# First two quads of an attention and projection kernel on two hardware queues, with a searched schedule

## The chip, the cores and the metric

One core of a Trainium2 chip. The time is the device time of one execution in microseconds (us), measured over whole launches; the profiled span is a little shorter than it. The kernel before takes 432.91 us (median of 3 runs, 432.63 to 433.24) and its profiled span is 431.5 us.

Engines in the text: PE is TensorE's matmul (PEld its weight load), ACT is ScalarE, DVE is VectorE, POOL is GpSimd, SP is SyncE, which only issues transfers here.

## The reference

```python
# q, k, v: (8 batches, 12 heads, 448 positions, 64), float32
def _attn_ref(q, k, v):
    scores = np.matmul(q, k.transpose(0, 1, 3, 2)) / np.sqrt(64)
    m = np.max(scores, axis=-1, keepdims=True)
    e = np.exp(scores - m)
    attn = e / (np.sum(e, axis=-1, keepdims=True) + np.exp(-m) + 1e-09)
    return np.matmul(attn, v)

# x: (3584 tokens, 768), w_in: (768, 2048), w_out: (2048, 768)
def _moe_ref(x, w_in, w_out, a, b):
    h = x @ w_in
    P = a[0] + a[1] * h + a[2] * h**2 + a[3] * h**3
    Q = 1.0 + abs(b[0]) * abs(h) + abs(b[1]) * h**2
    return (P / (Q + 1e-06)) @ w_out
# x is the attention's output, heads side by side; the result is (3584, 768) float32
```

## The kernel before

Each batch is worked as three "quads" of four heads. A quad's Q and K are loaded, transposed (by PE for the first six quads, later by DMA), multiplied into scores, put through Exp on ACT, and multiplied with ones (the sums) and with V (the values). A group of scores, its Exp and so on is an entry in a queue of its engine; `Plan` simulates the engines with fixed durations and writes the instructions in the order that this simulation gives. So the constants below are not measured at run time: they decide, when the kernel is built, in which order each engine works. PE has attention, first projection ("gemm1", `x @ w_in`) and second product ("gemm2", by `w_out`) to interleave; until the first sums of batch 0 are multiplied in, it has only attention.

```python
DUES = (0, 0, 4, 6); T0 = 18.0; T1 = 22.0; P1 = 1.3; LEAD = 45.0   # due times of a quad's scores
def quad_due(n):
    if n < 2 * NQ:
        return T1 + 8 * P1 * (n - NQ)
    return T0 + 8 * PER * (n - NQ)

def first_loads():                    # quad 0, in eight pieces of 112 KB, float32
    # ... piece(ti, pr, jh, nj, dma, lat, cast): ti 0 = K, 1 = Q; a load on queue `dma`
    #     into a stage, and a cast to float16 by the engine `cast`
    piece(0, 0, 0, 2, "ACT", 2.8, "ACT")
    piece(1, 0, 0, 2, "SP", 2.65, "DVE")
    piece(0, 0, 2, 2, "ACT", 3.4, "ACT")
    piece(1, 1, 0, 2, "SP", 3.9, "DVE")
    piece(0, 1, 0, 2, "ACT", 3.6, "ACT")
    piece(0, 1, 2, 2, "SP", 3.7, "ACT")
    for pr in range(2):
        piece(1, pr, 2, 2, "SP", 6.8, "DVE", True)     # second rows of Q, needed later

# ... transposes by PE: eight nc.tensor.transpose of 112 x 64 into one bank, one DVE copy out
# ... scores: tensor.matmul pairs on 64 rows each, Exp on ACT for 112 x 896 at a time
# ... attend: 16 sums, 2 x 16 values, Ln and Exp of the sums on ACT, two multiplies on DVE

# GpSimd's queue: quad 1 first (cast while loading), then the rest
kload.append(load_op(1, k, kn, "k", kfree, NN))
qload.append(load_op(1, q, qn, "q", qfree, NN))
loads(0, "v"); loads(2, "kq"); loads(1, "v"); loads(2, "v")
ORDER = "kq3 i kq4 i kq5 v3 i v4 i v5 o kq6 o o o"     # i, o: a group of weights
# ...
LAG = {0: (0, 2.67), 1: (5, 2), B - 2: (9, 2.67), B - 1: (8, 2)}   # places of second products
plan.run()
for op in plan.order:
    op.emit()
```

The softmax here doesn't subtract the row's maximum and nothing guards it: scores larger than these inputs give would overflow.

## Time and profile before

| | before |
|---|---|
| time, median of 3 | 432.91 us |
| profiled span | 431.5 us |
| PE busy | 419.2 us, 97% |
| ACT busy | 327.8 us, 76% |
| first Exp starts | 8.19 us |
| first sums start on PE | 13.93 us |
| first projection matmul starts | 27.30 us |
| from there to the end of the last second product | 400.9 us |

The page, the stretches of 5 us and the heads of the two timelines are shown in the prediction. Here is one more view, ACT's timeline between the first Exp and the first projection. The columns are start, busy time, engine, line, operation, out and in, shapes, number of instructions, and in brackets the idle time before the first of them and what ended it.

```profile
10.22 1.92 ACT L480 ACTIVATE e<-sps 112x896 f16<-112x896 f32 x2 [0.32 <-PE sps L472]
...
16.89 1.72 ACT L480 ACTIVATE e<-sps 112x896 f16<-112x896 f32 x2 [1.10 <-PE sps L472]
19.65 0.92 ACT L480 ACTIVATE e<-sps 112x896 f16<-112x896 f32 x1 [1.04 <-PE sps L472]
```

ACT waits for scores four times and for sums once, 3.5 us in all, before its chain runs dense from 19.65 us on.

### The profile page before, as it was taken

How to read it: one execution, taken by the hardware profiler on the slowest of the kernel's cores; microseconds unless marked ns; L12 is line 12 of the kernel's file. 1: busy time of each engine (PE TensorE's matmuls, PEld its weight loads, DVE VectorE, ACT ScalarE, POOL GpSimd, SP SyncE). 2: the span in 40 equal slices, each digit the busy share in tenths (PEclk: the TensorE clock that was granted, in tenths of full speed). 3: DMA queues.
4: the chain of work that ended last, by engine and by line, in shares of the span. 5: the costliest groups of instructions: out<-in, count | busy, mean ns of one | idle time of the engine just before them, and what ended most of it. 6: DMA issues, size and time to landing. Idle time of an engine off the chain costs nothing.

```text
span 431.5 us, 8834 instructions
## 1 busy us (share of the span) xinstructions
PE 419.2 (97%) x3680; PEld 218.7 (51%) x3680; DVE 339.9 (79%) x505; ACT 327.8 (76%) x386; POOL 120.7 (28%) x172
## 2 busy tenths in 40 slices
PE   3999999999999999999999999999999999999996
PEld 2667665544444444444454444444444455555563
DVE  2445999998999887698998668979698788999800
ACT  4699999798888777888886897877798854578521
POOL 5655516566005340423703333052000000000000
PEclk9999999999999999999999999999999999999999
DMA  9999999899606947299399886373211011111132
GB/s 148 202 200 205 207 180 150 152 154 162 123 2 69 160 85 118 28 141 115 58 117 107 119 123 85 81 108 73 45 36 38 2 36 38 36 38 36 39 103 81
DMA packets 78153, 43.12 MB, mean 100 GB/s; under 512 B 36128, under 2 KB 74528, under 8 KB 78112
## 3 DMA queue, kind: packets, MB, share of 16 engines
q0 software_dynamic: 37856, 22.35, 39.7%
q1 hardware_dynamic: 39472, 19.80, 25.5%
q8 instruction: 29, 0.48, 0.5%
q10 hardware_dynamic: 784, 0.39, 0.4%
q14 instruction: 12, 0.10, 0.1%
HBM read 45.62 MB, written 11.01 MB: 131 GB/s over the span
## 4 chain that ended last, share of the span: by engine, by line
PE 89%; ACT 4%; DMA 3%; DVE 1%; issue 1%; ACTq 0%; POOLq 0%
PE gen L671 34%; PE gen L573 33%; PE gen L507 12%; PE sps L472 10%; DMA kn<-in_k_dram 2%; ACT e L480 2%; DMA h<-in_k_dram 1%; ACT c L625 1%; ACT c L628 1%; PE gen L389 1%; DVE h L590 0%; ACT lden L521 0%; DVE x L535 0%; ACT lden L523 0%; DVE c L614 0%
## 5 line engine op out<-in xcount | busy, mean ns | idle before, releaser
L480 ACT ACTIVATE e<-sps 112x896 f16<-112x896 f32 x192 | 167.1, 917 | 41.5 <-PE sps L472 41.1
L573 PE MATMUL gen<-x,w_in 128*128 128x448 f16 (+1 forms) x864 | 161.8, 332 | 0.0
L671 PE MATMUL gen<-w_out,g 128*128 128x384 f16 (+2 forms) x768 | 135.9, 326 | 0.0
L573 PEld LDWEIGHTS <-w_in 128*128 128x128 f16 x864 | 79.9, 98 | 68.3 <-issue 14.4
L671 PEld LDWEIGHTS <-g 128*128 128x128 f16 x768 | 72.7, 98 | 58.4 <-issue 10.4
L590 DVE CAST h<-gen 128x448 f16<-128x448 f32 x113 | 69.4, 618 | 24.4 <-PE gen L573 24.3
L614 DVE TENSOR_TENSOR n<-n,h 128x1792 f16<-128x1792 f16 x64 | 70.1, 1095 | 0.7
L625 ACT ACTIVATE c<-c,oneeps_c 128x1792 f16<-128x1792 f16 x32 | 57.3, 1791 | 11.4 <-DVE c L614 11.1
L472 PE MATMUL sps<-qt,kt 64*128 64x448 f16 (+1 forms) x432 | 58.4, 343 | 2.3 <-ACT e L480 1.1
L648 POOL COPY gx<-g 128x1024 f16<-128x1024 f16 x8 | 8.3, 1040 | 183.1 <-DVE g L614 183.1
L693 ACT ACTIVATE o<-gen 128x384 f32<-128x384 f32 (+2 forms) x56 | 27.4, 490 | 36.2 <-PE gen L671 36.0
L628 ACT ACTIVATE c<-c 128x1792 f16<-128x1792 f16 x32 | 54.6, 1705 | 0.3
L610 DVE TENSOR_SCALAR n<-n,abc 128x1792 f16<-128x1792 f16 x64 | 44.3, 693 | 1.1
L614 DVE TENSOR_TENSOR g<-n,c 128x1792 f16<-128x1792 f16 x32 | 35.1, 1098 | 12.8 <-ACT c L628 11.5
L433 POOL COPY kp<-kn 112x256 uint32<-112x256 uint32 x36 | 26.1, 755 | 57.2 <-DMA kt<-kp 50.3
L507 PE MATMUL gen<-e,vn 112*32 112x448 f16 (+1 forms) x864 | 41.8, 337 | 0.0
L535 DVE TENSOR_TENSOR x<-gen,lden 128x448 f16<-128x448 f32 (+1 forms) x54 | 28.3, 563 | 13.9 <-ACT lden L523 12.7
L614 DVE TENSOR_TENSOR c<-c,w 128x1792 f16<-128x1792 f16 x32 | 35.2, 1100 | 0.0
L472 PEld LDWEIGHTS <-kt 64*128 64x128 f16 x432 | 15.0, 96 | 36.5 <-issue 32.9
L507 PEld LDWEIGHTS <-vn 112*32 112x32 f16 x864 | 23.1, 99 | 14.0
L433 POOL COPY qp<-qn 112x256 uint32<-112x256 uint32 x36 | 25.2, 726 | 18.1 <-DMA qt<-qp 18.0
L610 DVE TENSOR_SCALAR n<-h,abc 128x1792 f16<-128x1792 f16 x32 | 24.7, 772 | 0.1
(42 smaller groups left out, 248.1 us busy)
## 6 DMA issues: line engine op xcount, KB each, us to landing
vn<-in_v_dram POOLq DMA_DIRECT2D x24, 224.0 KB, 8.5
kn<-in_k_dram POOLq DMA_DIRECT2D x23, 224.0 KB, 5.7
qn<-in_q_dram POOLq DMA_DIRECT2D x23, 224.0 KB, 7.4
w_in<-in_moe_w_in_dram POOLq DMA_DIRECT2D x12, 256.0 KB, 9.7
w_out<-in_moe_w_out_dram POOLq DMA_DIRECT2D x4, 768.0 KB, 16.2
out_dram<-o SPq DMA_DIRECT2D x8, 336.0 KB, 3.2
out_dram<-o SPq DMA_DIRECT2D x8, 288.0 KB, 2.8
out_dram<-o SPq DMA_DIRECT2D x7, 240.0 KB, 2.5
```

The source lines that it names most:

```text
L433: nc.gpsimd.tensor_copy(out=mid[0].bitcast(U32)[:, pr], in_=src[n % NN].bitcast(U32)[:, 2 * pr:2 * pr + 2] .rearrange("p e j d -> p j e d"))
L472: nc.tensor.matmul(out=sps[m % NS][0:(P if i == 0 and j == 1 else 128), hh, ci * qw:(ci + 1) * qw], lhsT=kt[n % NK][r, c0:c0 + (P if i == ...
L480: nc.scalar.activation(out=e_sb[m % NE], in_=sps[m % NS][0:P, :, 0:S], func=AF.Exp, scale=scale)
L507: nc.tensor.matmul(out=gen[unit["bank"]][32 * h:32 * h + 32, 0:qw], lhsT=lhs(h, j), rhs=e_sb[m % NE][:, h % 2, c0:c0 + qw], start=(j == 0) ...
L535: mult.emit = lambda s=s, uu=uu: nc.vector.tensor_tensor(out=x_sb[b % NX][:, 2 * qd + s, q0:q0 + qw], in0=gen[uu["bank"]][:, 0:qw], in1=ld ...
L573: nc.tensor.matmul(out=gen[unit["bank"]][:, fi * qw:(fi + 1) * qw], lhsT=w_in_sb[wg][:, c // 2, c % 2, (fc % FG) * 128:(fc % FG + 1) * 128 ...
L590: nc.vector.tensor_copy(out=dst, in_=src)
L610: return lambda: nc.vector.tensor_scalar(out=out, in0=in0, scalar1=s1, scalar2=s2, op0=op0, **kw)
L614: return lambda: nc.vector.tensor_tensor(out=out, in0=in0, in1=in1, op=ALU.mult)
L625: lambda: nc.scalar.activation(out=c, in_=c, func=AF.Ln, bias=oneeps_c)))
L628: lambda: nc.scalar.activation(out=c, in_=c, func=AF.Exp, scale=-1.0)))
L671: nc.tensor.matmul(out=gen[unit["bank"]][:, 0:wd], lhsT=lhs, rhs=w_out_sb[f][:, fc % FG, cols], start=(fc == 0), stop=(fc == NFC - 1))
```

## The change

The intent: the first Exp comes earlier, since the first six pieces of Q and K meet no large load; quad 1 comes over the two hardware queues as float32 and is cast by DVE, while GpSimd's first load waits for a memset behind the first casts (`vz`); and from there on due times, the places of second products and the order of loads are found by search, against the plan's own model of the transfers (its constants are assumptions of the code).

```diff
-KB_US = 0.00252
+KB_US = 0.0027
+X_US = 1.3
+X_SHARE = 6.3
...
+    def transfer(self, op):
+        if op.kb < 0:
+            first = max(op.end + 0.3, self.ring)
+            behind = max(self.hbm - first, 0.0)
+            self.ring = first + X_US + min(behind, X_SHARE)
...
-    DUES = (0, 0, 4, 6)
-    T0 = 18.0
...
+    DUES = (0, 0, 4.2, 3.0)
+    LEAD = 50.9
+    DUE = (
+        28.1, 39.7, 51.4, 58.5, 76.4, 91.4, 103.2, 87.5, 118.5,
+        129.9, 148.0, 129.5, 202.0, 155.9, 169.8, 134.0, 237.8, 280.8,
+        283.4, 262.8, 327.3,
+    )
...
-        piece(0, 0, 0, 2, "ACT", 2.8, "ACT")
-        piece(1, 0, 0, 2, "SP", 2.65, "DVE")
-        piece(0, 0, 2, 2, "ACT", 3.4, "ACT")
...
+        plan.add("c0", piece(0, 0, 0, 2, "ACT", 2.8))
+        plan.add("c0", piece(1, 0, 0, 2, "SP", 2.65))
+        plan.add("c0", piece(0, 0, 2, 2, "ACT", 3.0, "ACT"))
+        piece(1, 1, 0, 2, "SP", 3.0)
+        piece(0, 1, 0, 2, "ACT", 3.4)
+        piece(0, 1, 2, 2, "SP", 3.4)
         for pr in range(2):
-            piece(1, pr, 2, 2, "SP", 6.8, "DVE", True)
+            for ti, (src, dst, dma) in enumerate(((k, kn, "ACT"), (q, qn, "SP"))):
+                stage = quad1_stage(ti, pr)
+                d = load(dma, src, 4 + 2 * pr, 2, stage, 0, J, 4.3 + 1.1 * pr)
+                cast(1, ti, pr, 0, J, dst[1][:, 2 * pr:2 * pr + 2], stage, d)
...
-    kload.append(load_op(1, k, kn, "k", kfree, NN))
-    qload.append(load_op(1, q, qn, "q", qfree, NN))
+    vz = plan.add("cpt", Op("vz", "DVE", 0.06, [first_casts[0, 1, 0, 0]],
+                            lambda: nc.vector.memset(vn[0][:, 0, 0, 0:2], 0.0)))
     loads(0, "v")
+    vload[0].deps.append(vz)
...
-    ORDER = "kq3 i kq4 i kq5 v3 i v4 i v5 o kq6 o o o"
+    ORDER = "kikiikivkkvoovoovkvv"
...
-            more = {-1: first[:2], 0: first[2:4], 1: first[4:], 2: nxt[:1], 3: nxt[1:2]}
+            more = {-1: first[:2], 0: first[2:3], 1: first[3:], 2: nxt[:2]}
...
-    LAG = {0: L0, 1: L1, B - 2: L6, B - 1: (8, 2)}
+    LAG = (
+        (0, 3.5), (12.0, 1.8), (6.5, 2.4), (5.0, 1.9),
+        (4.0, 3.4), (12.0, 1.8), (11.5, 2.8), (12.0, 1.3),
+    )
```

The rest of the diff is bookkeeping (lists turned into dictionaries, one load fewer in flight in the model).

## The prediction

> **What bounds the kernel now.** I read the page first, for which engine is full and where it is not:
>
> ```profile
> span 431.5 us, 8834 instructions
> PE 419.2 (97%) x3680; PEld 218.7 (51%) x3680; DVE 339.9 (79%) x505; ACT 327.8 (76%) x386; POOL 120.7 (28%) x172
> ...
> PE   3999999999999999999999999999999999999996
> ...
> PE 89%; ACT 4%; DMA 3%; DVE 1%; issue 1%; ACTq 0%; POOLq 0%
> ```
>
> PE is busy in 39 of 40 slices and holds 89% of the chain that ended last; DVE and ACT have a fifth to a quarter spare. Idle time lies in the first slice. Then busy time by stretches of 5 us (PE, PEld, DVE, ACT, POOL, clock, DMA share, GB/s):
>
> ```profile
> 0.00:5.00 5.00, 0.64 (x10) 0.52 (x12) 1.47 (x18) 2.12 (x3) 4.21 (x11) 1.00 0.50 123
> 5.00:10.00 5.00, 2.61 (x28) 1.21 (x27) 1.46 (x5) 2.33 (x4) 1.48 (x3) 1.00 1.27 167
> 10.00:15.00 5.00, 4.51 (x70) 2.99 (x72) 1.55 (x4) 3.63 (x5) 3.49 (x5) 1.00 1.38 200
> ```
>
> Half of the first 10 us is lost on PE, and by 15 us ACT has worked 8.1 us. The PE timeline shows what a busy PE does there:
>
> ```profile
> 8.03 0.40 PE L389 MATMUL gen<-ident,kn 112*64 112x112 f16 x4 [2.20 <-ACT kn L351]
> ...
> 12.18 0.93 PE L472 MATMUL sps<-qt,kt 64*128 64x224 f16 x8 [0.49 <-ACT e L480]
> ...
> 19.25 0.56 PE L472 MATMUL sps<-qt,kt 64*128 64x224 f16 x8
> ...
> 27.30 0.75 PE L573 MATMUL gen<-x,w_in 128*128 128x224 f16 x6
> ```
>
> The same eight score matmuls took 0.93 us at 12 us and 0.56 at 19 us: until about 18 us PE runs at half rate, though the page grants it the whole clock. The first projection matmul (L573) starts at 27.30; until then PE has only attention of batch 0 to do, and cannot be filled. What held ACT is in its own timeline, and the cause in the chain of the first 30 us:
>
> ```profile
> 4.41 0.42 ACT L351 ACTIVATE kn<-h 112x256 f16<-112x256 f32 x1 [0.47 <-DMA h<-in_k_dram]
> 7.56 0.72 ACT L351 ACTIVATE kn<-h 112x256 f16<-112x256 f32 x2 [2.74 <-DMA h<-in_k_dram]
> 8.19 1.70 ACT L480 ACTIVATE e<-sps 112x896 f16<-112x896 f32 x2
> ```
> ```profile
> 1.72 5.82 DMA h<-in_k_dram
> ...
> 10.01 8.87 DMA kn<-in_k_dram
> ```
>
> The first scores were written by 5.51 (PE starts them at 4.95), but ACT, in order, stood 2.74 us at a cast whose data landed only at 7.54. So the first exp began at 8.19.
>
> [...]
>
> **The change, part by part.** No matmul is added or removed. Array time is the same in both. At 2.4 GHz the first product is 8 x 16 x 6 x 448 columns = 143.36 us, the second the same, scores 35.84 (two row halves at once), sums and values 53.76 (four column groups), transposes 4.48: 380.8 us. Besides it PE pays for changes of kind: 9 projection matmuls from 203.97 to 205.68 pass into other projection matmuls almost without loss, but each step into or out of scores or values costs about 0.105 us (4 scores, 0.373 us of columns, take 0.48 to the next start). Counting steps in the built instruction order: 241 before, 234 after. That is 7 x 0.105 = 0.7 us gained, the whole of what the new places of second products can give by themselves.
>
> (a) Quad 1 goes from GpSimd's queue to the ACT and SP queues as f32, cast by DVE, and GpSimd's first load now waits for a DVE memset behind the first casts. So the six first pieces (0.69 MB) meet no large load. Pieces one to four landed by 4.4 in the trace; the other two should follow at about 5 instead of 7.2 to 7.5. Most casts go to DVE, which had worked 1.5 of 5 us; ACT keeps one cast, so nothing on it waits for a late piece. Against that, ACT issues two more DMAs (about 0.45 us each, from 0.74 to 2.2 now), so its table load of 1.28 us ends at 4.4 instead of 3.5: still before the first scores. First exp: about 5.7 instead of 8.19, a gain of 2.5 us.
>
> (b) From there ACT sets the pace until the first projection. In the built order that needs 14 exps and three pairs of ln and exp: 14 x 0.815 + 3 x (0.40 + 0.28) = 13.4 us, plus about 0.9 for PE and the last two multiplies. Before, 8.19 + 14.3 = 22.5 was possible and 27.30 came out: 4.8 us of slip, in ACT's gaps (1.10 and 1.04 us for scores) behind late loads and a PE at half rate. After, 5.7 + 14.3 = 20.0 is possible. Quad 2's Q and K are the second and third load of GpSimd instead of fourth and fifth. By the end of Q: 1.84 MB on the hardware queues and 3 x 0.459 MB; at the 0.39 MB/us that loads reach in the trace (one of 0.459 MB every 1.17 us) from 2.5 us on, 10.7 us against 14.54 now. The first weights: the same 6.6 MB in front of their last byte in both; 19.5 us by that rate against 23.45 measured. I leave a slip of 2.6 us for the half-rate PE and what isn't foreseen: first projection at **22.6**, a gain of 4.7.
>
> (c) From the first projection on PE has filling work. Before: 27.30 to 428.18 is 400.9 us, of which 370.9 are columns, 215 steps x 0.105 = 22.6, 1,760 projection matmuls x 2.5 ns = 4.4: 397.9. The rest, 3.0, is small losses and one hole of 1.1 us near 127 where ACT's exps were behind. After: 371.3 + 209 x 0.105 + 4.4 = 397.6. I put 2.4 for losses.
>
> Sum: 22.6 + 397.6 + 2.4 = 422.6; the last outputs as before, 431.5 - 428.2 = 3.3: span 425.9. Timed runs are 1.4 us over the profiled span (432.91 against 431.5): **427.3 us**, 1.3% faster.
>
> **Rivals.** First, the gain at the start is eaten by another wait. The weights may come late: between the first and the second weight group there are still Q and K of quad 4, and the sharing of quad 1's loads could slow everything else. For it: before 8.87 us only 1.15 MB had landed, well below the later rate, so the start isn't ruled by bytes alone. Against it: less is in flight in front of the bytes needed first. If the first projection stays at 25 or 26, the time is 430 to 431.
>
> Second, ACT becomes the bound later. The new due times pull attention forward. Weighing the instructions in program order with the durations of the trace, ACT has to do about 154 us by the time PE's own work reaches 160, against 144 before; in single 10 us stretches it is over 10. A hole like the one at 127 could come several times, 1 us each: 429 to 430. It speaks against this that in 40 to 60 us ACT was busy 9.3 and 9.9 of 10 us while PE had no gap.
>
> Third, it goes better: slip of only 1 us and losses down to 1 us. That gives 21.0 + 398.6 + 4.7 = 424.3, just at the line of 2%. Nothing else is there to take: without any loss after the start, and with PE full from 20 us, it is 422.
>
> **Range and chances.** The terms are independent: first projection 22.6 within about 1.5, losses 2.4 within about 1.5, and half a microsecond of run differences. That makes about 2.2 for one sigma-like error either way, and I widen it for the unforeseen: 424.2 to 430.6. Faster by over 2% (below 424.25) needs the third rival whole: 0.1. Slower by over 2% would need 9 us of new waits on a PE that has the same work: 0.01. Within 2%: 0.89.
>
> **What would show it.** First exp on ACT at 5.5 to 6.2; first projection on PE at 21 to 24; score groups of eight at 0.56 us from about 14 us instead of 19; PE's busy time in 5 to 10 us up from 2.61 to over 3.5. From the first projection to the last second product 399 to 401 us. If the first exp is near 8, step (a) is wrong; if it is early and the projection late, step (b); if the second length is over 402, ACT's holes are (c)'s fault and the waits of PE on scores will name them.

A paragraph is cut from the prediction where marked, since it restated rules that no run of this case had shown. 22.6 + 397.6 + 2.4 + 3.3 = 425.9, and 1.4 more is the 427.3. The trace of the kernel before shows this: K's first piece landed 2.7 us after its issue, and the third, issued at 1.72 us just behind GpSimd's first large load (1.49), took 5.8 us; that the large load held it up was the estimate. The column times of the sum can be read from the same trace: projection matmuls and second products of 224, 256, 384, 448 and 512 columns followed one another after 96, 109, 163, 189 and 216 ns (medians, at full rate). That is 0.417 ns for each column, the 2.4 GHz of the text, and 2.3 to 3.0 ns more for each matmul, the text's 2.5. The two matmuls of a pair of row halves (scores), and the four of a set of column groups (sums and values), started 3 ns apart (median).

## The result, and the profile after

The changed kernel takes 430.78 us (median of 4 runs, 430.65 to 431.20) against 432.77 for the kernel before in the same rounds (432.04 to 433.24, 4 runs). The ratio is 0.9957, 95% interval 0.9940 to 0.9974: 0.4% faster, where 1.3% was predicted. A ratio is here the mean time of one kernel's fast runs over the mean of the other's of the same rounds, so it is not quite the ratio of the two medians. The predicted class (within 2%) holds; the predicted time of 427.3 us and its range of 424.2 to 430.6 do not.

From the page of the kernel after: span and instructions, busy times, PE in 40 slices, and the chain by engine.

```profile
span 429.0 us, 8850 instructions
...
PE 418.3 (98%) x3680; PEld 218.5 (51%) x3680; DVE 339.7 (79%) x513; ACT 327.9 (76%) x383; POOL 109.3 (25%) x170
...
PE   5899999999999999999999999999999999999996
...
PE 81%; DVE 14%; ACT 2%; DMA 1%; issue 1%; ACTq 0%; DVEq 0%
```

Only the first two slices differ (5 and 8 in place of 3 and 9). The chain now passes through DVE for 14%, but no hole of PE belongs to that: PE is busy in all other slices as before. The busy times in stretches of 5 us (PE, PEld, DVE, ACT, POOL, clock, DMA share, GB/s) say where the early gain lies:

```profile
0.00:5.00 5.00, 0.60 (x8) 0.47 (x9) 1.48 (x21) 0.96 (x1) 1.17 (x7) 1.00 0.61 159
5.00:10.00 5.00, 4.08 (x48) 2.14 (x47) 3.11 (x12) 3.38 (x5) 4.80 (x8) 1.00 1.22 238
10.00:15.00 5.00, 4.55 (x76) 3.01 (x76) 2.01 (x6) 3.37 (x5) 3.06 (x5) 1.00 1.42 199
```

PE's busy time from 5 to 10 us rose from 2.61 to 4.08 us, with 48 matmuls against 28. From 10 to 15 us there is nothing left of it: 4.55 against 4.51. The ACT timeline shows the same from the other side:

```profile
4.04 1.28 ACT L775 ACT_TABLE_LOAD   x1 [4.04 <-DMA h<-in_k_dram]
5.33 0.42 ACT L365 ACTIVATE kn<-h 112x256 f16<-112x256 f32 x1
5.66 0.90 ACT L525 ACTIVATE e<-sps 112x896 f16<-112x896 f32 x1
7.17 0.92 ACT L525 ACTIVATE e<-sps 112x896 f16<-112x896 f32 x1 [0.62 <-PE sps L517]
8.61 0.92 ACT L525 ACTIVATE e<-sps 112x896 f16<-112x896 f32 x1 [0.53 <-PE sps L517]
10.17 2.53 ACT L525 ACTIVATE e<-sps 112x896 f16<-112x896 f32 x3 [0.64 <-PE sps L517]
13.51 0.45 ACT L566 ACTIVATE lden<-gen,one_c 128x224 f32<-128x224 f32 x1 [0.81 <-PE gen L552]
...
15.37 2.58 ACT L525 ACTIVATE e<-sps 112x896 f16<-112x896 f32 x3 [0.99 <-PE sps L517]
```

The first Exp starts at 5.66 instead of 8.19, but then ACT has a gap before each of the next three, where before they followed one another with a single gap of 0.32. The fourth starts at 10.17 instead of 11.22. PE's timeline from there:

```profile
9.57 1.12 PE L517 MATMUL sps<-qt,kt 64*128 64x224 f16 x8
...
12.51 0.94 PE L552 MATMUL gen<-e,ones 112*32 112x224 f16 x16
...
14.88 0.64 PE L517 MATMUL sps<-qt,kt 64*128 64x224 f16 x8
...
24.86 0.75 PE L618 MATMUL gen<-x,w_in 128*128 128x224 f16 x6
```

A group of eight scores costs 1.12 us at 9.57 (0.93 without the short pause inside it, as in the kernel before) and 0.64 at 14.88: half rate ends near 15 us instead of 18. The first projection matmul starts at 24.86, where 22.6 was predicted.

Because single profiles differ by several tenths, both kernels were profiled again unchanged (two more each):

> The changed kernel again, unchanged, for its profile. Clock theory: [...]the first projection follows it: at 24.7 to 25.0 if the half rate ends by 15.3, at 25.5 to 26.2 if it ends at 17 or later. Rival: the first projection is within 0.2 us of 24.86 whatever the clock does.

> The changed kernel once more, the same expectations: the first projection at 24.7 to 25.0 with a half rate that ends by 15.3, at 25.5 to 26.2 with one that ends at 17 or later; by the rival, 24.86 within 0.2 in any case.

> The kernel before again, unchanged, for its profile. In the one profile of it K's last pieces landed at 7.54 us and the first exp began at 8.19; three programs with its start landed them at 6.40 to 7.66. If that landing sets the first projection, each 0.1 us earlier of it is worth about 0.1 us, and the 27.30 of the first profile is a late one: first projection between 26.0 and 27.4. If not: 27.3 again.

> The kernel before once more, the same expectations: first projection between 26.0 and 27.4, the earlier the sooner K's last pieces land; 27.3 again if that landing does not set it.

Measured, in us, three profiles of each kernel. "Half rate until" is where the trace's clock record changes; "stretch after" runs from the first projection matmul to the end of the last second product; "tail" is what follows to the end of the span.

| | before | after | gain of the means |
|---|---|---|---|
| first Exp | 8.19, 8.13, 7.27 | 5.66, 5.41, 5.43 | 2.36 |
| fourth Exp | 11.22, 11.15, 10.29 | 10.17, 10.34, 10.32 | 0.61 |
| first sums | 13.93, 13.86, 13.01 | 12.51, 12.68, 12.67 | 0.98 |
| half rate until | 18.08, 18.23, 16.27 | 15.08, 17.30, 17.16 | |
| first projection | 27.30, 26.96, 26.59 | 24.86, 25.48, 25.41 | 1.70 |
| stretch after | 400.88, 401.19, 400.85 | 400.48, 400.39, 400.66 | 0.46 |
| tail | 3.33, 3.33, 3.32 | 3.65, 3.68, 3.67 | -0.34 |
| span | 431.5, 431.5, 430.8 | 429.0, 429.5, 429.7 | 1.82 |

(The times beside these four extra profiles were 431.32 and 431.51 after, 433.33 and 432.53 before.) The first projection of the changed kernel came at 25.48 and 25.41 with half rate until 17.30 and 17.16: just short of what the clock theory had expected (25.5 to 26.2), and outside the rival's 24.66 to 25.06. The kernel before came at 26.96 and 26.59, within its range: K's last piece landed at 7.54, 7.47 and 6.61 us in its three profiles, and the first sums followed 6.39 to 6.40 us later each time. The sum of the last gains, 1.70 + 0.46 - 0.34 = 1.82, answers to the 1.99 us between the medians. So the question is: 2.36 us are won at the first Exp; why are only 0.98 of them left at the first sums, and 1.70 at the first projection?

### The profile page after: what moved, and what is told of

The parts are those of the page before. It is cut to its first block, busy times and chain, and to the rows that moved or that the text cites. A ratio compares the mean times of both kernels' runs of the same rounds, so it can differ in the third digit from the quotient of the medians.

```text
span 429.0 us, 8850 instructions
## 1 busy us (share of the span) xinstructions
PE 418.3 (98%) x3680; PEld 218.5 (51%) x3680; DVE 339.7 (79%) x513; ACT 327.9 (76%) x383; POOL 109.3 (25%) x170
## 4 chain that ended last, share of the span: by engine, by line
PE 81%; DVE 14%; ACT 2%; DMA 1%; issue 1%; ACTq 0%; DVEq 0%
PE gen L716 33%; PE gen L618 29%; PE gen L552 11%; PE sps L517 8%; DVE h L635 3%; DVE n L655 2%; DVE n L659 2%; ACT e L525 2%; DVE c L659 1%; DMA g<-in_k_dram 1%; DVE g L659 1%; DVE x L580 1%; DVE c L655 1%; DVE w L655 1%; PE gen L433 0%
## 5 line engine op out<-in xcount | busy, mean ns | idle before, releaser
L693 POOL COPY gx<-g 128x1024 f16<-128x1024 f16 x8 | 9.4, 1172 | 154.7 <-DVE g L659 154.7
L318 POOL DMA_DIRECT2D vn<-in_v_dram x24 | 18.1, 755 | 57.4 <-PE sps L517 43.9
L478 POOL COPY kp<-kn 112x256 uint32<-112x256 uint32 x36 | 19.5, 573 | 44.5 <-DMA kt<-kp 41.4
L655 DVE TENSOR_SCALAR n<-h,abc 128x1792 f16<-128x1792 f16 x32 | 25.5, 797 | 0.3
```

The costliest lines, as they stand in the source:

```text
L655: return lambda: nc.vector.tensor_scalar(out=out, in0=in0, scalar1=s1, scalar2=s2, op0=op0, **kw)
```

## The experiments

All kernels gave the correct result. Each batch was timed beside the kernel before on the same chip: it had medians of 432.74, 432.86, 432.69, 432.93 and 432.86 us in the five timed batches.

**One part alone: the new start with the old schedule.** The diff is against the changed kernel.

```diff
-    DUES = (0, 0, 4.2, 3.0); LEAD = 50.9; TLEAD = 4.6; quad_due: DUE[n - NQ]
+    DUES = (0, 0, 4, 6); LEAD = 45.0; TLEAD = 5.0; quad_due: as before, from T0, T1, P1
-    ORDER = "kikiikivkkvoovoovkvv"
+    ORDER = "kikikvivivokooo"
-    LAG = ((0, 3.5), (12.0, 1.8), ...)
+    LAG = {0: (0, 2.67), 1: (5, 2), B - 2: (9, 2.67), B - 1: (8, 2)}
```

> The changed start (quad 1 on two hardware queues, casts on DVE, GpSimd's first load held back) with the old due times, old places of second products, old order of weight loads. Theory 1 (all of the gain is the earlier first projection, 24.86 against 27.30 us; the searched schedule gives only the 0.4 us seen after it): first projection within 0.5 us of 24.9, time about 0.4 us over the changed kernel, some 431.2. Theory 2 (the earlier start is worth something only because the new schedule uses it; with the old one it is lost in holes later): first projection also near 24.9, but the stretch from there to the last second product grows from 400.9 to about 402.5 and the time is near 432.5.

Measured: 436.51 us (435.78 to 440.03, 6 runs), ratio 1.0100 [1.0069, 1.0131]: slower than before. The first projection came at 25.73, 1.2 us earlier than before (mean 26.95), but the stretch after took 404.72 us. PE is idle there for 4.4 us in all (0.2 in the changed kernel): 1.76 us before 73.7, 0.57 near 103, and three gaps of 0.82, 0.44 and 0.55 between 132.5 and 135. The first, in PE's timeline:

```profile
73.71 0.37 PE L517 MATMUL sps<-qt,kt 64*128 64x448 f16 x2 [1.76 <-ACT e L525]
```

and in ACT's timeline at the same time:

```profile
70.30 1.71 ACT L673 ACTIVATE c<-c 128x1792 f16<-128x1792 f16 x1
...
72.73 2.54 ACT L525 ACTIVATE e<-sps 112x896 f16<-112x896 f32 x3
```

PE's scores wait for an Exp that stands on ACT behind an Exp of 1.71 us for the projection's quotient and two smaller instructions. The theory that the two parts simply add (431.2) falls; the one in which the old due times no longer fit the new start holds, and more strongly than it was put.

**The other part alone: the searched schedule with the old start.**

```diff
-        (quad 1 in first_loads on the ACT and SP queues, vz gate on GpSimd's first load)
+        (first_loads of before: six pieces with casts on ACT, quad 1 first on GpSimd's queue)
         DUE, DUES, LEAD, TLEAD, LAG, ORDER and the transfer model as in the changed kernel
```

> The old start with the new due times, places of second products, order of loads and model of the plan. Theory 1: first projection near 27.3, the stretch after it near 400.5, time 432.4, same as before within 0.5. Theory 2 (the schedule is what pays): 431 or less, with the stretch after the first projection at 399.5 or less.

Measured: 432.53 us (430.96 to 432.68, 6 runs), ratio 0.9979 [0.9963, 0.9995]; first projection 25.88, stretch after 401.61. Theory 1 had the time right, but by two errors that cancel. A part of the gain at the first projection comes without any change of the first loads: against the profile of the kernel before in which K's last piece landed as early (6.61 us, here 6.68), it is 0.7 us. A likely reason, not tested apart, is that the old order has 40 transposes in one group, which reach to quad 3's K, landing at 17 to 19 us (PE waited 0.37, 0 and 1.01 us for it in three profiles), and the new one 32. By the medians, start alone +3.8 us, schedule alone -0.2, both -2.0: the parts do not add. The stretch after the first projection is 4 us longer when the old schedule meets the new start, and 1 us longer when the new schedule meets the old start.

**Undo one part: quad 1 back on GpSimd's queue.**

```diff
-            for ti, (src, dst, dma) in enumerate(((k, kn, "ACT"), (q, qn, "SP"))):
-                ... load and cast of quad 1's four pieces
+    loads(1, "kq")                 # first on GpSimd's queue, cast while loading
+    kload[1].deps.append(vz)       # the gate stays
     loads(0, "v")
```

> The changed kernel with quad 1 put back on GpSimd's queue with the cast in the DMA (Q and K of quad 1 are its first two loads, still held back by the DVE memset); casts of quad 0 on DVE as changed. Theory C (writing f32 costs the DMA engines about twice what a casting load costs per element, so moving quad 1 to the hardware queues gained nothing by itself, and the gain is from holding back GpSimd and moving the casts): K's last pieces land at about 5.3 instead of 6.2 to 6.5, quad 1 at about 8 to 9.5, the first weights at about 22 instead of 23.24, first projection 24.9 or earlier, time 430.8 or up to 0.6 less. Theory D (the two hardware queues are what pays): quad 1 lands after 10, first projection at 26 or later, time 432 or more.

Measured: 434.06 us (433.0 to 435.71, 6 runs), ratio 1.0025 [1.0006, 1.0043]. ACT was free earlier (its table load ran from 2.22), but quad 1's Q, now one load, landed at 10.15, where the first half of it had landed at 7.7 to 8.0 in the changed kernel; the fourth Exp came at 11.31, first sums at 13.65, first projection at 25.92. The hardware queues are thus worth about 0.7 us at the first projection, and the theory that they only cost falls. The rest of the loss is a stretch after of 402.72, with PE idle for 1.3 us of it (the longest gaps 0.43 us near 48 and 0.52 near 127). That again a schedule doesn't fit its start is likely, but wasn't tested.

**ACT's own order: the table load ahead of two transfers.** In the changed kernel ACT issues five transfers first; the fifth issue is held until 3.7 to 4.0, so its table load runs from 4.04 and its one cast ends at 5.75. That cast feeds the second score group, and the second Exp waits 0.62 us.

```diff
+        table_op.append(plan.add("head", Op("table", "ACT", 1.3, [], ...)))   # before quad 1's loop
         for pr in range(2):
             for ti, (src, dst, dma) in enumerate(((k, kn, "ACT"), (q, qn, "SP"))):
```

> The changed kernel with ACT's table load ahead of its two loads of quad 1 instead of behind them. In the changed kernel the fifth issue held ACT till 4.01, the table load ended at 5.32, the cast of K's second piece ran 5.33 to 5.75, and the second exp waited 0.62 us. Theory A (this order is a cost of the change that I under-counted): cast at about 4.4, second exp at 6.5 instead of 7.17, first projection 0.5 us earlier, time 430.3. Theory B (the exps behind it are paced by K's last pieces at 6.2 to 6.5 and quad 1 at 8.2): second exp early, third exp still at 8.5 or later, first projection and time unchanged within 0.2.

Measured: 431.78 us (431.1 to 432.02, 5 runs), ratio 0.9967 [0.9953, 0.9982]. The second Exp came 0.4 us earlier (6.77), but quad 1's K landed at 8.99 instead of 8.18, and the fourth Exp at 11.10. Both theories missed: the first projection was later (26.14), not earlier or unchanged. What ACT did first gained 0.4 us, and what it issued behind that lost 0.8.

**Loads as float32 or with a cast: the cost by itself.** Three extra loads of 448 KB of source each, behind the first loads of the kernel before, once without and once with a cast to float16.

```diff
+    for i in range(3):     # into a tile that is free then; f32 probe: bitcast, f16 probe: cast
+        plan.add("load", Op(f"probe{i}", "POOL", 0.85, [], lambda i=i: nc.gpsimd.dma_start(
+            out=probe_tile(i), in_=v[7, 4 * i:4 * i + 4].rearrange(...)), kb=448))
```

> The kernel before with three more loads of 448 KB on GpSimd's queue behind the second V, written as f32 to an unused place: how long the DMA engines take for one, from the distance of their landings. If the rate is set by bytes written (about 200 GB/s at the destination in all of the first 60 us, and 245 to 286 while only f32 pieces ran): 1.6 to 2.3 us each. If it is set by bytes read: 1.17 us each, as for a casting load.

> The same with the three loads cast to f16 on the way. Either way 1.15 to 1.25 us each.

Measured (one look each, 441.35 and 439.49 us): the landings in the trace followed one another after 1.96, 1.87 and 1.98 us as float32, and after 1.23, 1.34 and 0.95 us with the cast. For 459 kB read that is 0.24 against 0.39 MB/us. So a float32 load took about 1.65 times as long as a casting load (1.94 against 1.17 us in the mean), whose rate the prediction took for everything. (This was measured on GpSimd's queue; that the float32 pieces of the two hardware queues go at the same rate is likely, not shown.) In the changed kernel, K's last pieces of quad 0 landed at 5.9 to 6.5 us (about 5 predicted), quad 1's first halves at 7.7 to 8.2, quad 2's Q at 12.6 to 13.0 (10.7 predicted) and the first weights at 22.5 to 23.25 (19.5 predicted; 22.5 to 23.5 before).

**PE's order: the fourth score group ahead of quad 1's transposes.**

```diff
     plan.run()
+    # op "s3" and behind it the first "t1" are moved to just after the next "cpt0"
+    o[j + 1:j + 1] = [s3, t1]
```

> The changed kernel with one move and nothing else: the fourth score group of quad 0 stands before, not behind, the first two transposes of quad 1 in PE's order. Theory of order (PE, in order, holds that score back until quad 1's K has landed at 8.18 and been cast, so the fourth exp starts at 10.17 with ACT idle 0.64 us before it): fourth exp at about 9.5, first projection 0.3 to 0.7 us earlier, time 430.2 to 430.5. Rival (PE at half rate has the same work to do until the first sums, so ACT's earlier exp only waits later): fourth exp early, but first sums still at about 12.5 and the first projection unchanged within 0.2.

Measured: 430.97 us (430.23 to 431.37, 6 runs), ratio 0.9958 [0.9943, 0.9973], the same as the changed kernel. ACT's timeline:

```profile
8.38 1.96 ACT L525 ACTIVATE e<-sps 112x896 f16<-112x896 f32 x2 [0.52 <-PE sps L517]
11.35 1.72 ACT L525 ACTIVATE e<-sps 112x896 f16<-112x896 f32 x2 [1.02 <-PE sps L517]
```

The fourth Exp now follows the third without a gap (9.42 instead of 10.17), but the gap only moves: the fifth waits 1.02 us. The first sums start at 12.51, to the hundredth where they were, and the first projection at 24.68, within the rival's 0.2. PE worked through the transposes of quad 1 from 9.31 on at half rate. The test is weaker than it looks: quad 1's K happened to land 0.4 us earlier here (7.80), and the moved scores still waited for a copy that stood on DVE behind quad 1's two casts until 8.50.

**PE's clock, five tries.** The theory under test: half rate before the first sums costs the chain about 2 us. First, 24 matmuls of the identity at the front of PE's queue, ahead of all data:

```diff
+        if i == 0:
+            plan.add("att", Op("warm", "PE", 2.5, [ident_op], lambda: [nc.tensor.matmul(
+                out=sps[1][:, 0, 0:128], lhsT=ident, rhs=ident, start=True, stop=True)
+                for _ in range(24)], mode="t"))
```

> The changed kernel with 24 matmuls of 128 x 128 on the identity put on PE at about 1.4 us, ahead of everything else; they write a score bank that is overwritten later, so the result is right. They keep the array busy from about 1.4 to 4.0 us. Clock theory (from the first transposes to 15.08 us PE runs at half rate, and from 8.7 to 15.3 us, where it stands full, that sets the pace): the half rate ends before 9 us, the first sums and values take 1.3 us instead of 2.36, first projection at 22.5 to 23.5 instead of 24.86, time 429.0 to 429.5. Rival (exps and landings pace the start, the slower PE hides behind them): the half rate ends early too, but the first projection stays within 0.4 us of 24.9 and the time within 0.4 of 430.8.

Measured: 431.49 us (430.77 to 431.96, 6 runs), ratio 0.9968 [0.9951, 0.9985]. PE's timeline:

```profile
1.36 2.74 PE L835 MATMUL sps<-ident 128*128 128x128 f16 x24 [1.36 <-POOL ident masks.py:199]
...
9.77 1.11 PE L517 MATMUL sps<-qt,kt 64*128 64x224 f16 x8
```

Half rate ended at 4.18 us and was back at 7.59, 3.41 us later, although PE was never idle for more than 0.46 us in between: eight scores at 9.77 took 1.11 us again. So the theory wasn't tested by this run. Next, eight more such matmuls before every early transpose or score group (two where the kind stays the same):

```diff
+        if early and op.eng == "PE" and op.name[0] in "ts" and seen is not None:
+            for _ in range(8 if seen.mode != op.mode else 2):
+                nc.tensor.matmul(out=bank, lhsT=ident, rhs=ident, start=True, stop=True)
```

> The warm-up of e5_warm kept up: besides the 24 matmuls at 1.4 us, 8 matmuls of 128 x 128 on the identity ahead of each early transpose or score group where PE changes kind (2 where it does not), into the bank that this group then overwrites, up to the second quad's sums. In e5_warm the half rate ended at 4.18 us and came back at 7.59[...]. Clock theory (the half rate from 8.7 to 15 us sets the pace of the start): full rate from about 4.2 without a relapse, first sums and values in 1.3 us instead of 2.36, first projection at 23.0 to 23.8 instead of 24.86, not earlier as the first weights land at 23.24; time 429.3 to 430.0. Rival (something else paces the start): full rate early, first projection still 24.5 or later, time 430.5 or more.

Measured: 435.89 us (435.02 to 437.0, 6 runs), ratio 1.0072. Full rate from 6.63 on and kept; but the groups of fillers, 0.3 to 0.6 us each at full rate, lay in the chain, and the first projection came at 29.95. Nothing follows for the theory.

Then transposes as plain matmuls by the identity, to see whether half rate ends sooner with them; alone, and with the 24 early matmuls:

```diff
-                                nc.tensor.transpose(tp[...], src[...], ident[0:P, 0:P])     # float16 in PSUM
+                                nc.tensor.matmul(out=tp[...], lhsT=src[...],                # float32 in PSUM
+                                                 rhs=ident[0:P, 0:P], start=True, stop=True)
```

> The changed kernel, with every transpose on TensorE issued as a plain matmul by the identity (float32 into the same PSUM bank) in place of transpose mode; the same number of matmuls, the same order. Theory A (the slip after the first exp is mostly the half rate[...]): half rate ends at 8 to 12 us instead of 14.6 to 17.3, first sums at 11.3 to 12.0 instead of 12.5 to 12.7, first projection at 22.8 to 24.0 instead of 24.7 to 25.5, time about 429.3. Theory B[...]: half rate still ends between 14.6 and 17.3, first projection 24.7 to 25.5, time 430.5 to 431.5. In both the copies out of PSUM may become slower, since they read float32; if they take 0.2 us more each, first sums come up to 0.3 us later.

> The same plain transposes with the 24 matmuls of the identity at the front, which released the clock at 4.18 us in the earlier run with transpose mode, where it fell back at 7.59. Theory A: released at about 4.2 and not lost again; first sums at 10.5 to 11.5, first projection at 22.5 to 23.5, time 428.5 to 429.5. Theory B: released at about 4.2, lost again near 7.6, full again after 14 us; first projection 24.7 to 25.7, time 430.5 to 431.5.

Measured: 433.65 us (432.55 to 434.73, 6 runs), ratio 1.0017, half rate until 17.69; and 433.15 us (432.71 to 434.42, 6 runs), ratio 1.0011, half rate until 15.75, without any early release. Half rate lasted as long with plain matmuls as with transposes (15.08 to 17.30 in the changed kernel's three profiles), so transpose mode is not what kept it here. (Eight transposes took 0.59 us at half rate and 0.36 at full rate, at 12.14 and 15.83 us of the last run below.) The 2.4 to 2.9 us lost against the changed kernel go with the copies out of PSUM, which read float32 now; nothing else was changed, though the schedule that no longer fits may be part of it. The groups of the changed kernel:

```profile
L441 DVE COPY kt<-gen 128x448 f16<-128x448 f16 x10 | 3.9, 385 | 5.5 <-PE gen L433 5.5
```

and of the one with plain transposes (busy us, mean ns, idle before):

```profile
L441 DVE CAST kt<-gen 128x448 f16<-128x448 f32 x10 | 6.2, 620 | 5.1 <-PE gen L433 5.0
```

620 ns instead of 385, and each score group behind transposes waits for two of them.

The traces show when the clock changed, not what in PE's work changed it. The same 24 early matmuls (1.36 to 4.10 us) were followed by the end of half rate at 4.18 us in the first of these runs and at 6.63 in the one with fillers, but only at 15.75 with plain transposes. In the profiles of the two kernels PE was busy without a gap just before half rate ended (all of 15.08 to 18.08 us before, and of 11.67 to 15.08 after), and for 3.22 and 2.85 of the 3.41 us from 8.26 to 11.67, at whose end it stayed. Full rate was lost in the first run after gaps of 0.46, 0.27, 0.37 and 0.36 us between 4.18 and 7.59, and kept in the changed kernel with PE busy for 3.07 of the 3.42 us from 15.08. No bound can be drawn from so few stretches. The expectation of the last run had a reading of the clock that goes beyond them; it is cut where marked, as are guesses at the cause in three of the other expectations.

The last try: the 24 early matmuls, and four fillers only ahead of the five score groups that follow transposes, where PE waits for a copy anyway.

```diff
+        if early and op.eng == "PE" and op.name[0] == "s" and seen.mode == "t":
+            for _ in range(4):
+                nc.tensor.matmul(out=sps[int(op.name[1:]) % NS][:, 0, 0:128],
+                                 lhsT=ident, rhs=ident, start=True, stop=True)
```

> The changed kernel with the 24 early matmuls of the identity and, before the sums of unit 0, four such matmuls ahead of each of the five score groups that follow transposes; there TensorE waits 0.2 to 0.4 us for a copy anyway. [...] Theory A ([...]half rate costs the chain after the first exp about 2 us): released between 4 and 8.3 us and not lost again; first sums at 11.0 to 12.0 instead of 12.5, first projection at 23.0 to 24.3 instead of 24.7 to 25.5, time 429.3 to 430.5. Theory B (the loads set the pace before the first sums, the clock does not): released early too, but first sums at 12.3 or later and first projection at 24.2 or later, time 430.5 to 431.5.[...]

Measured: 430.66 us (429.82 to 431.94, 6 runs), ratio 0.9948 [0.9934, 0.9963]: not to be told from the changed kernel (0.9957). Half rate ended at 5.03 us and came back at 11.86, and ended again at 15.27. The expectation that the clock would not be lost failed. PE's timeline in the stretch at full rate:

```profile
8.97 0.39 PE L433 MATMUL gen<-ident,kn 112*64 112x112 f16 x8 [0.57 <-DVE kn L364]
...
10.12 0.60 PE L517 MATMUL sps<-qt,kt 64*128 64x224 f16 x8
11.49 0.37 PE L517 MATMUL sps<-qt,kt 64*128 64x224 f16 x4 [0.78 <-ACT e L525]
...
12.65 0.94 PE L552 MATMUL gen<-e,ones 112*32 112x224 f16 x16
```

Eight scores took 0.60 us at 10.12 instead of 1.12, and yet the first sums started at 12.65, as in the unchanged kernel's profiles (12.51 to 12.68). What PE saved it spent waiting: 0.57 us for the cast of quad 1's K, 0.78 for an Exp. K's first half landed at 8.46 here, 0.2 to 0.3 later than in the changed kernel's profiles, so a saving of that size is hidden: from quad 1's first Q transposes to the first sums it took 3.18 us instead of 3.45. So 6.8 us of full rate before the first sums, with fillers of 0.40 us in them, bring about 0.3 us there; Theory B holds, and "half rate costs the chain 2 us" is refuted for that stretch.

**Weights earlier, and weights earlier with fillers.**

```diff
-    ORDER = "kikiikivkkvoovoovkvv"
+    ORDER = "ikkiikivkkvoovoovkvv"      # the second of the two has the fillers at every step as well
```

> The changed kernel with that order of loads alone, no warm-up. In the changed kernel the weights land at 23.24, 1.6 us before the first projection needs them, so this alone should give nothing: first projection 24.5 to 25.2, time 430.3 to 431.3. If the weights are what sets it after all: 23.5 or earlier, 429.5.

> The same with the first group of weights loaded ahead of quad 3's Q and K instead of behind them, so that it should land at about 20.9. If both the clock and then the weights hold the first projection: it comes at 22 to 23, time 428.5 to 429.5. If the order of loads only moves the wait to quad 3's transposes: no better than e12_warm_fill.

Measured: 433.21 us (432.71 to 433.43, 4 runs), ratio 1.0009 [0.9991, 1.0027], and 437.65 us (437.17 to 438.19, 4 runs), ratio 1.0113. The first weights landed at 21.0 instead of 22.5 to 23.3, so the weights were not what the first projection waited for: it came at 28.41, and at 31.61 with the fillers. Quad 3's K landed at 22.0 instead of 17.3 to 18.4. The plan also put a fourth group of sums on PE ahead of the first projection, so this is no change of loads alone.

## Why the prediction was wrong, point by point

**Step (a), the first Exp, was right:** 5.4 to 5.7 us measured, 5.7 predicted, and for the reason given: no wait of ACT for a late piece. Two figures beside it were off without harm there: the table load ended at 5.3, not 4.4, and pieces five and six landed at 5.9 to 6.5, not 5.

**Step (b) failed: "From there ACT sets the pace until the first projection", with "a slip of 2.6 us for the half-rate PE and what isn't foreseen".** The term is the delay of the chain from first Exp to first projection beyond 14.3 us. It measured 4.9, 5.8 and 5.7 us, and 4.8, 4.5 and 5.0 before. I had let it shrink by 2.2 because the loads would come early enough; it grew by 0.7. That is 2.3 us of the missed 3.5 in the profile beside the prediction (24.86 against 22.6), and 2.7 in the mean of three. ACT did not set the pace before the first sums: it stood idle before each of the next three Exps (0.62, 0.53 and 0.64 us). The runs split the slip at the first sums:

| mean us | before | after | change |
|---|---|---|---|
| first Exp to first sums | 5.74 | 7.12 | +1.38 |
| first sums to first projection | 13.35 | 12.63 | -0.72 |

*Ahead of the first sums* the chain is paced by what comes after the first pieces. Before, the first Exp was so late that all of quad 0 had landed with it (7.5 us), and four Exps ran with one gap; after, the first Exp ran ahead of its followers. K's last pieces, quad 1's float32 pieces with their DVE casts, and ACT's order each hold the next group. The chain of the changed kernel goes through quad 1 (from the chain of its first 26 us: start, us, what):

```profile
2.22 5.96 DMA g<-in_k_dram
...
8.20 0.44 DVE kn L364
...
8.68 0.96 PE gen L433 x16
```

The prediction has no landing of quad 1 at all. By its rate of 0.39 MB/us, the 1.15 MB up to quad 1's first half would have landed at about 5.4 us (an estimate, from 2.5 us on as in the prediction); they landed at 8.2. What follows is nearly fixed: in the ten profiles with the same order on PE from there to the first sums and half rate all the way, the sums start 3.45 to 3.47 us after quad 1's first Q transposes, which start at 8.93 to 10.20. So a later quad 1 delays the sums one for one, as the run with the table load first showed (K 0.8 us later, sums 0.8 to 0.9). An earlier one alone would gain less: PE stood only 0.11 to 0.38 us for it in the three profiles of the changed kernel. Beyond that the experiments show no single bound: the table load earlier made it later (through quad 1's landing), one score group earlier moved the gap by one Exp, and full rate turned mostly into waits for casts and Exps; first sums stayed at 12.5 to 13.5 us in all of them, and at 13.65 with quad 1 on GpSimd's queue. What it takes to bring them forward, loads, order and clock together, was not tried.

*Behind the first sums* the clock seems to count. In eight profiles with the changed start and the same order of work on PE from the first sums on (one has one filler group in it; the two with plain transposes are left out, since their copies are slower), the length of this stretch goes with how long half rate lasts after the sums' start:

| run | half rate left after first sums | first sums to first projection |
|---|---|---|
| score group earlier | 2.12 | 12.17 |
| quad 1 on GpSimd | 2.35 | 12.27 |
| after | 2.57 | 12.35 |
| fillers in the waits | 2.62 | 12.37 |
| table load earlier | 4.13 | 12.70 |
| after, third profile | 4.49 | 12.74 |
| after, second profile | 4.62 | 12.80 |
| early matmuls | 5.11 | 12.98 |

That is 0.27 us for each us of half rate between the first and the last row (0.24 by a fitted line), and between the three profiles of the changed kernel it is the end of half rate that differs (15.08, 17.30 and 17.16 us). The schedule alone has this order too, and fits (4.01 and 12.81). An estimate from these rows: without any half rate behind the first sums the stretch would take about 11.6 to 11.7 us, so half rate costs 0.6 to 1.2 us there in the changed kernel. No run took the half rate out of this stretch alone. In the profile beside the prediction, the predicted 22.6 would have needed that part whole (0.7) and some 1.6 more ahead of the sums.

In the same step, the rate of 0.39 MB/us was measured on casting loads and applied to float32 pieces; float32 loads ran at 0.24 in the probe. Besides quad 1, that set the landings of quad 2's Q two us too early and those of the weights three; but the landing of the weights was not what the first projection waited for.

**Step (c) was nearly right.** The stretch after measured 400.4 to 400.7, where 400.0 was predicted and 399 to 401 was to be expected; its gain of 0.46 is 0.3 from the counts (397.9 against 397.6) and 0.2 from losses. The losses were 2.8 to 3.1 us, as before (3.0), where 2.4 were put. The steps of kind, at about 0.105 us each, are some 25 us of the 431 in 241 steps (an estimate from the prediction's count). ACT did not become the bound, as the second rival feared: PE waits for Exp 1.2 us in all, nearly all of it ahead of the first projection. The "hole of 1.1 us near 127", on which that rival was built, was a wrong reading: PE's gap there is 0.44 us, at 128.3. Another was that "half of the first 10 us" is lost on PE: by the lines shown it is busy for 3.25 of them, so two thirds are.

**The tail and the offset.** The last outputs took 3.65 to 3.68 us instead of 3.33; why is open. It goes with the changed start (3.55 to 3.70 in every program that has it), not with the schedule (3.30 with the old start). And the offset of timed over profiled was taken as 1.4 from a median of three and a span of one; the profiled run itself had 433.28 us, so it was 1.8. Together 0.7 us. With the last 0.5 of step (c) and the 2.3 of step (b): 3.5.

**The rivals.** The first one had happened in its size ("if the first projection stays at 25 or 26, the time is 430 to 431"), though the first of its reasons, late weights, was wrong. The second, that "the sharing of quad 1's loads could slow everything else", holds in part: with quad 1 off the hardware queues, K's last pieces landed at 5.8 and 6.0 us instead of 5.9 to 6.5. The third, 424, was never near: it would have needed loads, order and clock ahead of the first sums to give way together.

Of the versions run, none beats the changed kernel beyond the intervals; two (score group earlier, fillers in the waits) equal it.

## What to carry to other kernels

Pulling the first instruction of a chain forward gains only as much as the next inputs come forward with it: predict when the fourth item and its data come, not the first, and let a delay shrink only if a view shows which wait goes away. A schedule that was searched belongs to the start it was searched with: half of such a change can be slower than none of it (1.0% here). And a rate read from one kind of transfer should not be put on another: 0.39 and 0.24 MB/us in the same kernel.
